# Mask additions laid out as one a chunk, equal score pieces side by side, and centring one batch later in a fused attention and gated FFN kernel

## The chip, the cores and the metric

The kernel runs on one core of a Trainium2 chip. A core has five engines that run their own instruction streams and wait for each other through semaphores: TensorE (PE, matmul, with its weight loads shown apart as PEld), VectorE (DVE), ScalarE (ACT), GpSimd (POOL) and SyncE (SP, which here issues DMA transfers). The metric is the device time of the whole program in microseconds (us).

## The reference

The input is x, 2048 tokens of 512 values. With xn = layernorm(x), the output is x + A(xn) * silu(B(xn)); A is sliding-window attention, B a gated feed-forward network. All weights are multiplied by 8.

```python
def _A_ref(x, wqkv, wo):                 # x: 1 x 2048 x 512
    H = 32; Dh = D // H; W = 256         # 32 heads of 16
    qkv = (x @ wqkv).reshape(B, S, 3, H, Dh).transpose(2, 0, 3, 1, 4)
    q, k, v = qkv[0], qkv[1], qkv[2]
    scores = jnp.einsum("bhqd,bhkd->bhqk", q, k) * (Dh ** -0.5)
    mask = (idx[:, None] - idx[None, :] >= 0) & (idx[:, None] - idx[None, :] < W)
    p = softmax(jnp.where(mask[None, None], scores, -1e9))
    o = jnp.einsum("bhqk,bhkd->bhqd", p, v)
    return o.transpose(0, 2, 1, 3).reshape(B, S, D) @ wo

def _B_ref(x, w1, w3, w2):               # F = 1792
    return (silu(x @ w1) * (x @ w3)) @ w2

xn = layernorm(x)
return x + _A_ref(xn, wqkv, wo) * silu(_B_ref(xn, w1, w3, w2))
```

## The kernel before

**Tiles.** The tokens are cut into four tiles t of 512; the 32 heads into four groups g of eight, and each group into two halves p of four heads. One (t, g, p) is a *unit* of attention: 32 units, eight of them in tile 0. Float32 products with the weights are made as three float16 products of high and low parts, so tensors come in pairs (XH and XL, wvh and wvl).

**A unit.** A first pass (L661 on PE, L675 on DVE) finds the largest score of each row. A second pass computes scores with the keys held in the array and the queries moving (`scores`, L742), adds masks to them on DVE (L749), exponentiates them on ACT (L752), and multiplies by the values (`values`, L770, float32). A unit of tiles 1 to 3 has five *chunks*, each filling one pair of PSUM banks of 2 x 512 columns: chunk 0 for both heads a of a row group, then two A chunks and two B chunks, one for each a. The chunk table CHUNKS gives, for each half h of the partitions, pieces (m, k, n, o, flag): key block m of 64 keys is multiplied with n blocks of 64 queries from block m + k on, and the result starts at block o of the chunk. Tile 0 has a table of its own, FIRST, with four chunks. The last tuple of a chunk lists its masks: at which block, every how many blocks, how many, and which entry of the constant table MK is added. MK holds triangles of 0 and a large negative number.

A score matmul uses a quarter of the array (64 x 64: half h, row group r), a value matmul an eighth (64 rows x 32 columns), so that four, or eight, run side by side. `values` takes the first piece of each half, then the second, and so on.

**The order of work.** PE's order is the order in which the code is written. A plan of batches puts the attention units between dense pieces: projections (L593, L563), gate and up of the FFN (L1032, L1257), the folded down projection (L1175) and the sum (L1309). The other engines' orders come from a scheduler that follows priorities; `urgent()` raises the priority of what is issued inside it, and `issue_after` names an instruction to stay behind. Queues hold work that is issued some steps later (`later`) or beside a batch: `behind` gives one work item to each batch of scores.

**Token statistics.** `prepare(t)` loads the four 128-token blocks of a tile, takes mean and variance on DVE (`stats`), computes the reciprocal root of the variance (`rstd`: a first guess on DVE, L442 to L447, then Newton steps, for tile 0 on DVE at L450 to L458, for later tiles as ten operations on POOL, L463 to L472), centres and scales the block on DVE (`centre`, L475), and transposes it on PE (`turn_beside`, L513). `prepare_beside` makes a list of these as work items. Also on DVE stand `L614`, which makes the low part of a projected tile, and L1281, which applies a scale to FFN results; the matmuls of L1257 use a slot or PSUM bank that such work has to free.

**The head.** For tile 0 the weights' powers of two are found first: sums of squares on ACT (L249), cast on DVE (L261), summed over partitions on PE, and turned into scales on DVE (L291 to L304). keep_busy (L1533) issues matmuls whose results nobody reads. Projected q and k go to DRAM (dQ, dK: L617 to L621) and come back in another layout (KA, qa: L637). L394 loads the raw weights of one head group, q and k.

Of the kernel before, what the change touches and what calls it, by code (L numbers as in the profile page):

```python
# [21 lines left out]
P = 128  # L22
# [47 lines left out]
AB = ((0,), (1,))  # L70
CHUNKS = (((0, 1), ((4, 0, 4, 0, 1),), ((-1, 1, 4, 0, 1),), ((0, 3, 2, 2, 0),)),
          *((a, ((0, 0, 5, 0, 1), (-2, 2, 3, 5, 1)), ((1, 0, 5, 0, 1), (5, 0, 3, 5, 1)),
             ((0, 4, 2, 0, 0), (5, 2, 2, 1, 0))) for a in AB),
          *((a, ((2, 0, 5, 0, 1), (6, 0, 2, 5, 1), (-4, 4, 1, 7, 1)), ((3, 0, 5, 0, 1), (7, 0, 1, 5, 1), (-3, 3, 2, 6, 1)),
             ((0, 4, 2, 0, 0), (5, 2, 2, 0, 0))) for a in AB))

FIRST = (*((a, ((0, 0, 5, 0, 1), (6, 0, 2, 5, 1), (4, 3, 1, 7, 1)), ((1, 0, 5, 0, 1), (5, 0, 3, 5, 1)),
            ((0, 4, 2, 0, 0), (5, 1, 1, 0, 0))) for a in AB),
         *((a, ((2, 0, 5, 0, 1), (4, 0, 3, 5, 1)), ((3, 0, 5, 0, 1), (7, 0, 1, 5, 1), (3, 1, 2, 6, 0)),
            ((0, 4, 2, 0, 0), (5, 1, 1, 0, 0))) for a in AB))  # L80


@with_exitstack
def tile_block(ctx: ExitStack, tc: tile.TileContext, x, wqkv, wo, w1, w3, w2, out):
# [124 lines left out]

    MK = const.tile([P, 3, 2, 64], BF16, name="MK")  # L210
    nc.vector.memset(MK[0:64], 0.0)
    for i, k in ((0, 0), (0, 1), (1, 1), (2, 0)):
        m = MK[0:64, i, k, :]
        nc.gpsimd.affine_select(m, m, pattern=[[-1 if k else 1, 64]], base=0, channel_multiplier=1 if k else -1,
                                compare_op=ALU.is_gt if k else ALU.is_ge, fill=NEG)

# [208 lines left out]
    def prepare(t):  # L425
# [14 lines left out]
        def rstd(b0, b1):  # L440
# [21 lines left out]
            u = lnpool.tile([P, b1 - b0], F32, name="u")  # L462
            pool.tensor_mul(sq, r0, r0)  # L463
            pool.tensor_mul(sq, sq, ve)
            pool.tensor_scalar(u, sq, -10 / 3, None, op0=ALU.add)
            pool.tensor_mul(sq, sq, u)
            pool.tensor_scalar(sq, sq, 5.0, None, op0=ALU.add)
            pool.tensor_mul(r0, r0, sq)
            pool.tensor_mul(sq, r0, r0)
            pool.tensor_mul(sq, sq, ve)  # L470
            pool.tensor_scalar(sq, sq, -0.5 * (3 / 8)**3 * XS, 1.5 * (3 / 8) * XS, op0=ALU.mult, op1=ALU.add)
            pool.tensor_mul(rs[:, b0:b1], sq, r0)  # L472

# [247 lines left out]
    def pass2(t, g, p):  # L721
# [3 lines left out]
        chunks = CHUNKS if t else FIRST  # L725

        def pieces(c):

# [7 lines left out]
        def scores(c):  # L736
            qa, ka = QA[t, g], keys(t, g)
            s = scores_bank()
            for o, h, a, (m, k, n, _, _) in pieces(c):
                for r in range(2):  # L740
                    rows = slice(64 * r, 64 * r + KR + 2)
                    nc.tensor.matmul(s[64 * h:64 * h + 64, r, o:o + 64 * n], ka[rows, 2 * p + a, 64 * (m + 4):64 * (m + 5)],  # L742
                                     qa[rows, 2 * p + a, 64 * (m + k):64 * (m + k + n)], start=True, stop=True)
            which, *_, masks = chunks[c]
            sv = s.rearrange("p r (a k q) -> p (r a) k q", a=len(which), q=64)
            for first, by, n, kind, of in masks:
                v = sv[:, :, first:first + by * (n - 1) + 1:by, :]
                with urgent():
                    nc.vector.tensor_add(v, v, MK[:, kind, of:of + n, :].unsqueeze(1).to_broadcast([P, 2 * len(which), n, 64]))  # L749
            cell[c] = pt = ppool.tile([P, 2, 512], F32, name="pt")  # L750
# [5 lines left out]
        def values(*cs):  # L756
# [8 lines left out]
            for group in zip_longest(*(turns[k] for k in sorted(turns))):  # L765
                for c, o, h, a, (m, k, n, _, _) in filter(None, group):
                    for r in range(2):
# [905 lines left out]
```

## Time and profile before

| | us |
|---|---|
| median of 3 runs (lowest, highest) | 818.14 (816.59, 819.52) |
| the profiled execution | 817.82 |
| its span in the profile | 816.0 |
| PE busy | 795.2 |
| DVE busy | 633.9 |
| ACT busy | 392.4 |
| POOL busy | 364.0 |

A row of the timeline reads: start in us, length in us, engine, line of the kernel, operation, output<-input by the program's names, the size of the array tile used (PE), the shape, the number of instructions in the row; in brackets the idle time ahead of it on its engine, and what ended it. Neighbouring instructions of one line stand in one row under the shape of the first, and the ends of matmuls overlap the starts of the next, so that for PE differences of starts are used. A row of the groups has, after the count, busy time and mean ns of one, and then the idle time before the group with what ended it. The stretches give busy time by engine and the granted clock of PE as a share of full speed.

### The profile page before, as it was taken

Reading aid. Unit: us, or ns where it says so; the run is one execution under the profiler, and the core shown is the slowest. Engines: PE = TensorE matmul, PEld = TensorE weight load, DVE = VectorE, ACT = ScalarE, POOL = GpSimd, SP = SyncE. Lnnn points to the kernel's source line nnn. Section 1 sums busy time; section 2 is a strip of 40 time slices with the busy share of each in tenths; the row PEclk is TensorE's granted clock in tenths of the full one; section 3 lists DMA queues with packets and bytes.
Section 4 is the critical chain, followed back from the end, with each engine's and each line's share of the span. In section 5 each row is a group of like instructions: output and inputs, shape, how many; then the busy total and the mean of one; then the engine's idle time right before and its main releaser. Section 6 shows DMA issues by size and latency. Waiting matters only on the chain.

```text
span 816.0 us, 23868 instructions
## 1 busy us (share of the span) xinstructions
PE 795.2 (97%) x9176; PEld 404.2 (50%) x9176; DVE 633.9 (78%) x2037; ACT 392.4 (48%) x591; POOL 364.0 (45%) x648
## 2 busy tenths in 40 slices
PE   8999989998999999999999999999999999999998
PEld 4434444443444444444444544456544654466465
DVE  8788788885898777787988888786777887775437
ACT  6879586563527444444444344434444334344421
POOL 2234266232328636434445264630246377560670
PEclk9999999999999999999999999999999999999999
DMA  9967554735457384666755544646362545325321
GB/s 284 258 218 254 165 179 130 276 115 188 136 141 255 105 267 120 215 180 208 204 169 171 172 100 144 168 128 189 122 197 74 161 127 149 111 77 181 111 56 70
DMA packets 109794, 134.18 MB, mean 164 GB/s; under 512 B 18864, under 2 KB 64880, under 8 KB 109680
## 3 DMA queue, kind: packets, MB, share of 16 engines
q1 hardware_dynamic: 109392, 132.13, 53.9%
q8 instruction: 72, 1.18, 0.6%
q10 hardware_dynamic: 288, 0.52, 0.2%
q14 instruction: 42, 0.34, 0.1%
HBM read 91.23 MB, written 36.57 MB: 157 GB/s over the span
## 4 chain that ended last, share of the span: by engine, by line
PE 78%; DVE 10%; ACT 5%; DMA 3%; issue 3%; SPq 1%; POOL 1%; DVEq 0%; POOLq 0%; ACTq 0%
PE m L1032 29%; PE po L770 8%; PE m L1257 8%; PE m L1175 8%; PE m L593 7%; PE s L742 5%; PE m L1309 4%; PE m L563 4%; PE s L661 3%; DVE junk L675 2%; PE po L661 2%; DMA slot<-in_A_x_dram 1%; DMA dW<-slot 1%; DVE s L749 1%; ACT slot L342 1%
## 5 line engine op out<-in xcount | busy, mean ns | idle before, releaser
L1032 PE MATMUL m<-XH,slot 128*128 128x512 f16 x896 | 267.5, 380 | 1.8 <-DVE slot L614 1.2
L752 ACT ACTIVATE pt<-s,es 128x1024 f32<-128x1024 f32 x152 | 167.6, 1112 | 198.6 <-DVE s L749 183.1
L339 POOL TENSOR_TENSOR slot<-slot,slot 128x256 f16<-128x256 f32 (+1 forms) x170 | 112.9, 691 | 218.2 <-ACT slot L1065 79.2
L1032 PEld LDWEIGHTS <-slot 128*128 128x128 f16 x1344 | 124.8, 98 | 156.2 <-issue 12.7
L1032 PE MATMUL m<-XL,slot 128*128 128x512 f16 x448 | 169.9, 379 | 0.0
L749 DVE TENSOR_TENSOR s<-s,MK 128x256 f32<-128x256 f32 (+2 forms) x280 | 118.7, 434 | 52.7 <-PE s L742 48.5
L675 DVE CUSTOM_DVE_ANT_0 junk<-s,MW 128x320 bf16<-128x320 f32 x276 | 133.9, 485 | 18.0 <-PE s L661 10.3
L675 DVE CUSTOM_DVE_ANT_0 junk<-po,MW 128x320 bf16<-128x320 f32 x172 | 83.4, 485 | 4.3
L1257 PE MATMUL m<-slot,slot 128*128 128x512 f16 x336 | 80.0, 385 | 3.6 <-DVE slot L614 3.2
L770 PE MATMUL po<-pt,V 64*32 64x320 f32 (+4 forms) x2880 | 77.2, 342 | 0.8 <-DVE pp L304 0.8
L593 PE MATMUL m<-XH,slot 128*128 128x512 f16 x240 | 71.0, 380 | 1.5 <-DVE slot L1051 0.8
L1175 PE MATMUL m<-slot,slot 128*128 128x256 f16 x588 | 68.4, 273 | 0.0
L1090 POOL TENSOR_TENSOR slot<-slot,slot 128x256 f16<-128x256 f32 x98 | 64.6, 671 | 1.1
L1047 ACT ACTIVATE slot<-m,sgs 128x512 f32<-128x512 f32 x56 | 38.3, 683 | 54.4 <-PE m L1032 53.1
L770 PEld LDWEIGHTS po<-pt,V 64*32 64x32 f32 x2880 | 50.5, 106 | 22.9 <-PE s L513 0.9
L1175 PEld LDWEIGHTS <-slot 128*128 128x128 f16 x588 | 56.1, 98 | 11.5 <-issue 2.8
L1051 DVE SCALAR_TENSOR_TENSOR slot<-slot,m 128x512 f32<-128x512 f32 x56 | 38.4, 685 | 27.9 <-ACT slot L1047 27.8
L742 PE MATMUL s<-qa,KA 50*64 50x320 f16 (+3 forms) x1472 | 58.6, 260 | 0.3 <-DVE M L675 0.2
L593 PEld LDWEIGHTS <-slot 128*128 128x128 f16 x384 | 35.6, 98 | 44.7 <-issue 3.3
L742 PEld LDWEIGHTS <-KA 50*64 50x64 f16 x1472 | 30.3, 106 | 52.5 <-issue 31.1
L1257 PEld LDWEIGHTS <-slot 128*128 128x128 f16 x336 | 30.9, 98 | 42.7 <-issue 8.9
L661 PE MATMUL s<-KA,qa 48*64 48x320 f16 (+3 forms) x824 | 45.1, 295 | 3.7 <-ACT pt L752 2.9
(188 smaller groups left out, 1095.3 us busy)
## 6 DMA issues: line engine op xcount, KB each, us to landing
slot<-dW SPq DMA_DIRECT2D x98, 256.0 KB
slot<-in_B_w_dram SPq DMA_DIRECT2D x56, 256.0 KB
slot<-dFold SPq DMA_DIRECT2D x48, 256.0 KB
dW<-slot SPq DMA_DIRECT2D x42, 256.0 KB
slot<-in_A_x_dram SPq DMA_DIRECT2D x30, 256.0 KB
KA<-dK SPq DMA_DIRECT2D x24, 288.0 KB
qa<-dQ SPq DMA_DIRECT2D x32, 192.0 KB
slot<-dWQ SPq DMA_DIRECT2D x24, 256.0 KB
```

The costliest lines, as they stand in the source:

```text
L339: op(out[:, c], a[:, c], b[:, c])
L593: nc.tensor.matmul(cell["pp"], w[:, (a * NC + c) * P:(a * NC + c + 1) * P], b[:, c, :], start=(c, i) == parts[0][0], stop=(c, i) == parts[ ...
L661: nc.tensor.matmul(s[c:c + w, r, :n], qa[rows, 2 * p + a, ii * P + c:ii * P + c + w], ka[rows, 2 * p + a, e - n:e], start=True, stop=True)
L675: lasts["maximum"] = nc.vector.tensor_tensor_reduce(out=junk[:, :n], in0=s[:, r, :n], in1=mask, scale=1.0, scalar=NEG, op0=ALU.add, op1=AL ...
L742: nc.tensor.matmul(s[64 * h:64 * h + 64, r, o:o + 64 * n], ka[rows, 2 * p + a, 64 * (m + 4):64 * (m + 5)], qa[rows, 2 * p + a, 64 * (m + k ...
L749: nc.vector.tensor_add(v, v, MK[:, kind, of:of + n, :].unsqueeze(1).to_broadcast([P, 2 * len(which), n, 64]))
L752: lasts["exp"] = nc.scalar.activation(pt, s, AF.Exp, scale=es)
L770: nc.tensor.matmul(cell["po"][32 * i:32 * i + 32, h, 64 * (m + k):64 * (m + k + n)], V[64 * h:64 * h + 64, (4 * t + m // 2) % VB, hd * VW: ...
L1032: nc.tensor.matmul(cell[k], w[:, (a * NC + c) * P:(a * NC + c + 1) * P], b[:, c, :], start=c == 0 and i == 0, stop=c == NC - 1 and i == 2)
L1090: nc.gpsimd.tensor_sub(lo, view, hi)
L1175: nc.tensor.matmul(cell["ps"][:, c], made[:, f:f + P], wj[:, g:g + 256], start=j == j0 and c == 0 and n == 0, stop=j == j1 - 1 and n == 2, ...
L1257: nc.tensor.matmul(ps, hh[:, a * TW + b * P:a * TW + (b + 1) * P], w[:, c * D:(c + 1) * D], start=f == f0 and i == 0, stop=f == f1 - 1 and ...
```

## The change

**Masks.** The mask table MK becomes eight entries of 64 columns, and each chunk's masks become one DVE addition: two places of n blocks each, against two runs of neighbouring entries of MK (chunk 0: one place). For that the blocks that need a mask have to lie next to each other, so some pieces are computed with their 64-query blocks in reverse order: a flag of -1 makes `turned_about` read the moving operand's blocks from last to first, in `scores` and again in `values`; outputs are written straight. In each unit of tiles 1 to 3 these are both heads' pieces of 256 columns of chunk 0 (half 1), a 192-column piece of each A chunk (half 0) and a 128-column piece of each B chunk (half 1). Tile 0's masks keep their shapes. The upper half of the table is built in MB on partitions 0 to 63 and copied by one DMA instead of three; POOL makes nine selections instead of four.

**B chunks.** The pieces of the B chunks stand in another order, so that in both halves they are 64, 320 and 128 columns wide.

**Statistics.** The ten POOL operations of `rstd` are issued as urgent, and for tiles 2 and 3 an empty work item stands between `rstd` and the first `centre`.

```diff
-CHUNKS = (((0, 1), ((4, 0, 4, 0, 1),), ((-1, 1, 4, 0, 1),), ((0, 3, 2, 2, 0),)),
-          *((a, ((0, 0, 5, 0, 1), (-2, 2, 3, 5, 1)), ((1, 0, 5, 0, 1), (5, 0, 3, 5, 1)),
-             ((0, 4, 2, 0, 0), (5, 2, 2, 1, 0))) for a in AB),
-          *((a, ((2, 0, 5, 0, 1), (6, 0, 2, 5, 1), (-4, 4, 1, 7, 1)), ((3, 0, 5, 0, 1), (7, 0, 1, 5, 1), (-3, 3, 2, 6, 1)),
-             ((0, 4, 2, 0, 0), (5, 2, 2, 0, 0))) for a in AB))
+CHUNKS = (((0, 1), ((4, 0, 4, 0, 1),), ((-1, 1, 4, 0, -1),), ((0, 1, 1, 7),)),
+          *((a, ((0, 0, 5, 0, 1), (-2, 2, 3, 5, -1)), ((1, 0, 5, 0, 1), (5, 0, 3, 5, 1)),
+             ((0, 4, 2, 0),)) for a in AB),
+          *((a, ((-4, 4, 1, 0, 1), (2, 0, 5, 1, 1), (6, 0, 2, 6, 1)), ((7, 0, 1, 0, 1), (3, 0, 5, 1, 1), (-3, 3, 2, 6, -1)),
+             ((0, 5, 2, 4),)) for a in AB))
...
+MASKS = ((1, 1), (0, 0), (2, 2), (2, 1), (2, 1), (1, 1), (2, 2), (1, 2))
...
+    MK = const.tile([P, len(MASKS), 64], BF16, name="MK")
+    MB = const.tile([64, len(MASKS), 64], BF16, name="MB")
+    for h, made in enumerate((MK[0:64], MB)):
+        nc.vector.memset(made, 0.0)
...
             pool = nc.gpsimd
             u = lnpool.tile([P, b1 - b0], F32, name="u")
-            pool.tensor_mul(sq, r0, r0)
...
+            with urgent():
+                pool.tensor_mul(sq, r0, r0)
...
         work.append(lambda: rstd(0, 4))
+        if t > 1:
+            work.append(lambda: None)
         work += [lambda bs=bs: [centre(b) for b in bs] for bs in pairs]
...
+        def turned_about(a, way):
+
+            return a.rearrange("p (n q) -> p n q", q=64)[:, ::-1, :] if way < 0 else a
...
                     nc.tensor.matmul(s[64 * h:64 * h + 64, r, o:o + 64 * n], ka[rows, 2 * p + a, 64 * (m + 4):64 * (m + 5)],
-                                     qa[rows, 2 * p + a, 64 * (m + k):64 * (m + k + n)], start=True, stop=True)
+                                     turned_about(qa[rows, 2 * p + a, 64 * (m + k):64 * (m + k + n)], way), start=True, stop=True)
...
-            sv = s.rearrange("p r (a k q) -> p (r a) k q", a=len(which), q=64)
-            for first, by, n, kind, of in masks:
-                v = sv[:, :, first:first + by * (n - 1) + 1:by, :]
+            sv = s.rearrange("p r (a w) -> p (r a) w", a=len(which))
+            for first, by, n, kind in masks:
+                places = 2 if by > 1 else 1
+                v = sv[:, :, 64 * first:64 * (first + n)]
+                if places == 2:
+                    v = type(v)(v.tensor, v.offset, [v.ap[0], v.ap[1], [64 * by, places], *v.ap[2:]])
+                    mk = MK[:, kind:kind + 2 * n, :].rearrange("p (i n) q -> p i (n q)", i=2)
+                else:
+                    mk = MK[:, kind:kind + n, :].rearrange("p n q -> p (n q)")
                 with urgent():
-                    nc.vector.tensor_add(v, v, MK[:, kind, of:of + n, :].unsqueeze(1).to_broadcast([P, 2 * len(which), n, 64]))
+                    nc.vector.tensor_add(v, v, mk.unsqueeze(1).to_broadcast([P, 2 * len(which), *mk.shape[1:]]))
...
-                                         cell[c][64 * h:64 * h + 64, r, o:o + 64 * n],
+                                         turned_about(cell[c][64 * h:64 * h + 64, r, o:o + 64 * n], way),
...
-    for i, k in enumerate((0, 2, 1)):
-        nc.sync.dma_start(MK[64:P, i], MK[0:64, k])
+    nc.sync.dma_start(MK[64:P], MB)
```

The lines of the changed kernel are up to 21 higher than those of the kernel before: `centre` is L484 there, `rstd` on POOL L472 to L481, the low part L625, the mask addition L770 and the value matmul L791. In the rows below an x and a count stand for so many such instructions in a row.

PE, the value matmuls of one unit of the later tiles, without their weight loads (po is the output, pt the exponentials, V the values). Before:

```order
L770 MATMUL po<-pt,V 32x256 x8
L770 MATMUL po<-pt,V 32x320 x8
L770 MATMUL po<-pt,V 32x192 x8
L770 MATMUL po<-pt,V 32x320 x8
L770 MATMUL po<-pt,V 32x128 x4
L770 MATMUL po<-pt,V 32x64 x8
L770 MATMUL po<-pt,V 32x128 x4
```

After:

```order
L791 MATMUL po<-pt,V 32x256 x8
L791 MATMUL po<-pt,V 32x320 x8
L791 MATMUL po<-pt,V 32x192 x8
L791 MATMUL po<-pt,V 32x64 x8
L791 MATMUL po<-pt,V 32x320 x8
L791 MATMUL po<-pt,V 32x128 x8
```

The pieces of 64 and 128 columns of the two halves no longer mix; the rest of PE's order stays, but for the score matmuls of the B chunks.

DVE, tile 2, around the first centring of its statistics (mv and rs are mean and reciprocal root). Before:

```order
L675 ISA junk,M<-po,M_106 128x256
L675 ISA M 128x1
L475 TENSOR_SCALAR slot_2653<-slot_2653,mv,rs 128x512
L614 SCALAR_TENSOR_TENSOR slot_3243<-m_3188,slot_3243 128x512
L1281 SCALAR_TENSOR_TENSOR slot_1458<-m_3248,dsc,slot_1458 128x512
L749 TENSOR_TENSOR s<-s,MK 128x4x64
```

After, at the same place:

```order
L686 ISA junk,M<-po,M_106 128x256
L686 ISA M 128x1
L625 SCALAR_TENSOR_TENSOR slot_3257<-m_3203,slot_3257 128x512
L1302 SCALAR_TENSOR_TENSOR slot_1473<-m_3262,dsc,slot_1473 128x512
L770 TENSOR_TENSOR s<-s,MK 128x4x64
```

The centring has left this place and stands behind a maximum of the next batch; the low part (L614, now L625) follows the maximum directly.

POOL, the second half of the ten operations for tile 2. Before:

```order
L467 TENSOR_SCALAR sq<-sq 128x4
L841 CAST slot_3259<-on 128x256
L468 TENSOR_TENSOR r_3152<-r_3152,sq 128x4
L841 CAST slot_3259<-on 128x256
L469 TENSOR_TENSOR sq<-r_3152 128x4
L339 TENSOR_TENSOR slot_3259<-on,slot_3259 128x256
L470 TENSOR_TENSOR sq<-sq,ve 128x4
L339 TENSOR_TENSOR slot_3259<-on,slot_3259 128x256
L471 TENSOR_SCALAR sq<-sq 128x4
L472 TENSOR_TENSOR rs<-sq,r_3152 128x4
```

After:

```order
L477 TENSOR_TENSOR r_3167<-r_3167,sq 128x4
L862 CAST slot_3273<-on 128x256
L478 TENSOR_TENSOR sq<-r_3167 128x4
L862 CAST slot_3273<-on 128x256
L479 TENSOR_TENSOR sq<-sq,ve 128x4
L347 TENSOR_TENSOR slot_3273<-on,slot_3273 128x256
L480 TENSOR_SCALAR sq<-sq 128x4
L347 TENSOR_TENSOR slot_3273<-on,slot_3273 128x256
L481 TENSOR_TENSOR rs<-sq,r_3167 128x4
```

The ten operations stand a place further ahead among the others; the last one still follows the two casts and the two L339 (now L347) operations.

DVE, the head, around the cast of the weights' sums (L261, now L269). Before:

```order
L447 TENSOR_SCALAR r_292<-r_292 128x4
L450 TENSOR_TENSOR sq<-r_292 128x4
L451 TENSOR_TENSOR sq<-sq,ve 128x4
L453 SCALAR_TENSOR_TENSOR sq<-sq 128x4
L454 SCALAR_TENSOR_TENSOR r_292<-sq,r_292 128x4
L261 CAST sb<-ssq 128x2
L456 TENSOR_TENSOR sq<-r_292 128x4
```

After:

```order
L269 CAST sb<-ssq 128x2
L458 TENSOR_TENSOR sq<-r_307 128x4
L459 TENSOR_TENSOR sq<-sq,ve 128x4
L299 TENSOR_SCALAR al<-s 128x1
L461 SCALAR_TENSOR_TENSOR sq<-sq 128x4
L306 TENSOR_SCALAR al<-al 128x1
L462 SCALAR_TENSOR_TENSOR r_307<-sq,r_307 128x4
```

The cast has moved ahead of the four Newton steps, and operations on the scale (al) stand between them.

SP, the head, around the first stores of dK and dQ. Before:

```order
L864 DMA slot_214<-in_B_w_dram 128x4x128
L621 DMA dK_147<-slot_408 128x512
L617 DMA dQ_143<-slot_417 128x2x512
L620 DMA dK_147<-slot_408 128x2x512
L618 DMA dQ_143<-slot_417 128x512
L394 DMA slot_551<-in_A_wqkv_dram 128x4x128
L621 DMA dK_148<-slot_462 128x512
```

After:

```order
L885 DMA slot_229<-in_B_w_dram 128x4x128
L402 DMA slot_566<-in_A_wqkv_dram 128x4x128
L402 DMA slot_567<-in_A_wqkv_dram 128x4x128
L632 DMA dK_164<-slot_423 128x512
L628 DMA dQ_160<-slot_432 128x2x512
L631 DMA dK_164<-slot_423 128x2x512
L629 DMA dQ_160<-slot_432 128x512
```

Two loads of weights now precede the stores; one of them stood right behind the four stores before, the other further on.

More of the change, by code (lines that the diff above doesn't have):

```diff
@@ L207, in tile_block @@
                             compare_op=ALU.is_ge, fill=NEG)
[L210 to L215, printed above, removed]
+    MK = const.tile([P, len(MASKS), 64], BF16, name="MK")
+    MB = const.tile([64, len(MASKS), 64], BF16, name="MB")
+    for h, made in enumerate((MK[0:64], MB)):
+        nc.vector.memset(made, 0.0)
+        kinds = [k[h] for k in MASKS]
+        for i, k in enumerate(kinds):
+            if k and (i == 0 or kinds[i - 1] != k):
+                n = next((j for j in range(i, len(kinds)) if kinds[j] != k), len(kinds)) - i
+                m = made[:, i:i + n, :]
+                nc.gpsimd.affine_select(m, m, pattern=[[0, n], [-1 if k == 2 else 1, 64]], base=0,
+                                        channel_multiplier=1 if k == 2 else -1,
+                                        compare_op=ALU.is_gt if k == 2 else ALU.is_ge, fill=NEG)
     NM = [const.tile([P, 64], F16, name=f"NM{i}") for i in range(3)]
@@ L738, in scores @@
             s = scores_bank()
-            for o, h, a, (m, k, n, _, _) in pieces(c):
+            for o, h, a, (m, k, n, _, way) in pieces(c):
                 for r in range(2):
@@ L765, in values @@
             for group in zip_longest(*(turns[k] for k in sorted(turns))):
-                for c, o, h, a, (m, k, n, _, _) in filter(None, group):
+                for c, o, h, a, (m, k, n, _, way) in filter(None, group):
                     for r in range(2):
```

22 lines of the change are left out of this document (11 added, 11 removed).

## The prediction, made before the changed kernel ran

> **What bounds the kernel now.** I read the page's busy line and chain first, then the stretches by stage, then single waits on the timeline.
>
> ```profile
> span 816.0 us, 23868 instructions
> PE 795.2 (97%) x9176; PEld 404.2 (50%) x9176; DVE 633.9 (78%) x2037; ACT 392.4 (48%) x591; POOL 364.0 (45%) x648
> PE 78%; DVE 10%; ACT 5%; DMA 3%; issue 3%; SPq 1%; POOL 1%; DVEq 0%; POOLq 0%; ACTq 0%
> ...
> 0.00:40.00 40.00, 36.16 (x201) 16.76 (x202) 31.74 (x112) 30.09 (x59) 11.29 (x41) 1.00 0.98 269
> 165.00:245.00 80.00, 75.38 (x831) 35.48 (x830) 65.16 (x232) 33.87 (x48) 22.80 (x44) 0.98 0.50 147
> 245.00:520.00 275.00, 274.78 (x3420) 131.16 (x3418) 223.92 (x699) 125.54 (x167) 141.64 (x246) 1.00 0.57 174
> 520.00:750.00 230.00, 229.81 (x2902) 128.98 (x2891) 173.43 (x536) 93.90 (x121) 103.40 (x174) 1.00 0.48 141
> ```
>
> The stretches list, after their length, the busy time of PE, its weight loads, DVE, ACT and POOL, then granted clock, DMA share and GB/s. From 245 to 750 us PE is busy 274.78 + 229.81 = 504.59 of 505.00 us. There only fewer or shorter PE instructions gain; a lighter DVE gains nothing. Before 245 PE has gaps, 4.62 us of them in the stretch from 165, and there order and waits count. So each part of the change is asked: does it shorten PE's own work, or close a gap before 245?
>
> **Part 1: the token statistics of tile 2.** The gap of the second stretch:
>
> ```profile
> 186.52 2.10 PE L1257 MATMUL m<-slot,slot 128*128 128x512 f16 x9
> 191.83 2.72 PE L1257 MATMUL m<-slot,slot 128*128 128x512 f16 x6 [3.20 <-DVE slot L614]
> ...
> 190.63 0.55 DVE L475 TENSOR_SCALAR slot<-slot,mv,rs 128x512 f32<-128x512 f32 x1 [3.40 <-POOL rs L472]
> 191.09 0.68 DVE L614 SCALAR_TENSOR_TENSOR slot<-m,slot 128x512 f16<-128x512 f32 x1
> ...
> 187.09 0.59 ACT L610 ACTIVATE slot<-m 128x512 f16<-128x512 f32 x1
> ...
> 190.40 0.20 POOL L472 TENSOR_TENSOR rs<-sq,r 128x4 f32<-128x4 f32 x1
> ...
> 191.80:194.60 2.80, 2.77 (x10) 0.84 (x13) 0.63 (x1) 0.00 (x0) 0.00 (x0) 0.50 0.70 233
> 133.96 1.40 PE m L1257 x6
> ```
>
> The DVE's first centring (L475) waits 3.40 us for the reciprocal root that POOL finishes at 190.60. Behind it in DVE's order stands L614, whose input ACT had ready at 187.09 + 0.59 = 187.68; PE waits for L614 and idles 3.20. Then the granted clock is 0.50, and six matmuls take 2.72 us; the same six took 1.40 in the chain's row at 133.96. So the wait costs 3.20 + 1.32 = 4.52 us.
>
> By the Trainium skill (TensorE: Matmul & The Clock Gate, Part 1: The HAM clock gate), the clock halves after an idle window of about 3.4 us and comes back after about as much busy time. The 0.50 of the row above agrees; nothing in the sum rests on this.
>
> The change puts the centring one work item, that is one batch of scores, later. The three batches between the first centring (190.63) and the fourth, which starts at 204.7, make 14.1 us, so one batch is about 4.7. The centring then comes at about 190.6 - 3.4 + 4.7 = 192 or later, after 190.60, and L614 can start at 187.7, before PE runs dry at 191.83 - 3.20 = 188.63: 187.7 + 0.68 = 188.4. What is late next is the transposes of tile 2, which start at 216.2: the fourth centring moves from 204.7 to about 209 and still precedes them. The urgent mark on POOL's ten operations leaves the last one behind the same four long operations, so I count nothing for it; if POOL still ended at 190.60, the batch of delay covers it alone. I take -4.5 (from -3.2, if the slow clock comes anyway, to -4.8).
>
> **Part 2: mask additions.** By shape, the groups of L749:
>
> ```profile
> L749 DVE TENSOR_TENSOR s<-s,MK 128x256 f32<-128x256 f32 x224 | 92.8, 427 | 52.5 <-PE s L742 48.5 <-issue 1.1 <-PE s L694 1.0
> L749 DVE TENSOR_TENSOR s<-s,MK 128x512 f32<-128x512 f32 x24 | 16.6, 691 | 0.0
> ```
>
> A unit of tiles 1 to 3 has eight additions of 427 ns and one of 691, 4.11 us; after, four of 691 and one of 427, 3.19 us. That is 0.92 x 24 = 22 us of DVE, and nothing on the path: PE is busy throughout 245 to 750, and DVE works 223.92 of 275.00 there. Tile 0 keeps its shapes. I take 0.
>
> **Part 3: values with equal pieces side by side (the B chunks).** One unit's value matmuls, row by row, and a change from 64-row tiles to the full array without it:
>
> ```profile
> 649.91 0.45 PE L770 MATMUL po<-pt,V 64*32 64x320 f32 x8
> 650.44 0.51 PE L770 MATMUL po<-pt,V 64*32 64x192 f32 x16
> 650.77 0.45 PE L770 MATMUL po<-pt,V 64*32 64x320 f32 x8
> 651.31 0.40 PE L770 MATMUL po<-pt,V 64*32 64x128 f32 x16
> 651.93 0.28 PE L1175 MATMUL m<-slot,slot 128*128 128x256 f16 x1
> ...
> 640.47 0.31 PE L661 MATMUL s<-KA,qa 48*64 48x320 f16 x4
> 640.62 0.30 PE L661 MATMUL po<-KA,qa 48*64 48x320 f16 x4
> 640.85 0.39 PE L1175 MATMUL m<-slot,slot 128*128 128x256 f16 x2
> ```
>
> Starts to starts: 320 columns 0.53, 192 equal columns 650.77 - 650.44 = 0.33, and the mixed last group (128 beside 64, then 64 beside 128; also 192 columns a half) 651.93 - 651.31 = 0.62. The last step holds the change to the full array: L661 alone takes 0.15 (640.47 to 640.62), followed by L1175 0.23 (to 640.85), so 0.08, at most 0.10. With equal pieces the group should take 0.33 + 0.10 = 0.43: -0.19 a unit, x 24 units = -4.6 us, all in stretches where PE is the bound. The least I allow is 0.12 (the small pieces keep a cost of their own), the most 0.24 (the 64-wide pieces hide in the long ones): -2.9 to -5.8.
>
> The Trainium skill (TensorE: Matmul & The Clock Gate, Part 3: Packing small matmuls) says that matmuls start and end strictly in program order. By it alone the mixed group would pay for 128 + 128 instead of 128 + 64 columns, 0.107 us at the 192-column row's rate, and the saving would be 2.6. The row's 0.62, against 0.43, says that more is lost, so I stay with 4.6.
>
> **Part 4: scores of the B chunks.** Two chunks' 24 score matmuls:
>
> ```profile
> 644.23 0.64 PE L742 MATMUL s<-qa,KA 50*64 50x320 f16 x24
> 644.76 0.33 PE L661 MATMUL po<-KA,qa 48*64 48x320 f16 x4
> ```
>
> They take 0.53; 1024 columns at the rate of the 512-column rows below (0.215) are 0.43. So at most 0.10 is to be had a unit (-2.4), and a narrow first piece could cost something: L661's 320 columns took 0.15 where 320 at that rate are 0.13, and that 0.02 to 0.03 a unit makes +0.7. I take 0, nearest the row: the work is the same.
>
> **Part 5: operands read back to front.** Chunk 0, A and B of every unit now read some moving operands in blocks of 64 columns from last to first. No row shows a reversed operand. The nearest is a matmul whose moving operand jumps back after every 128 columns (L1533 reads the same 128 columns four times), beside one that reads straight on:
>
> ```profile
> 12.79 1.02 PE L1533 MATMUL m<-onesb 128*128 128x512 bf16 x4 [0.58 <-DVE XL L499]
> 13.65 1.03 PE L593 MATMUL s<-XH,slot 128*128 128x512 f16 x4
> ```
>
> Four take 13.65 - 12.79 = 0.86, 0.215 each. L593's next group starts 0.86 later as well. Jumps cost nothing there; I take 0. The dear end is a rival below.
>
> **Part 6: the head.** DVE's order in the head changes, one cast (L261) standing ahead of the Newton steps:
>
> ```profile
> 8.25 0.19 ACT L249 ACTIVATION_READ_ACCUMULATOR sqa<-slot 128x1 f32 x1
> ...
> 7.95 0.16 DVE L450 TENSOR_TENSOR sq<-r 128x4 f32<-128x4 f32 x1
> 8.14 0.16 DVE L451 TENSOR_TENSOR sq<-sq,ve 128x4 f32<-128x4 f32 x1
> 8.62 0.16 DVE L261 CAST sb<-ssq 128x2 bf16<-128x2 f32 x1
> 9.57 1.91 DVE L475 TENSOR_SCALAR slot<-slot,mv,rs 128x512 f32<-128x512 f32 x4
> ```
>
> The cast needs ACT's sum, 8.25 + 0.19 = 8.44. Ahead of L450 it holds that back from 7.95 to about 8.5, and the rest of the chain goes 0.19 a step (7.95 to 8.14) as before; some of the scale operations between also move up. So centring starts 0.5 later, on the way to PE's first projection: +0.5.
>
> SP: three mask transfers become one, and two 256 KB weight loads (L394) that stood behind the first stores of dK and dQ now stand ahead of them.
>
> ```profile
> 21.41 1.34 SPq L394 DMA_DIRECT2D slot<-in_A_wqkv_dram  x1
> 24.62 0.82 SPq L637 DMA_DIRECT2D KA<-dK  x2
> 30.32 0.30 PE L661 MATMUL s<-KA,qa 48*64 48x128 f16 x7 [0.59 <-DMA qa<-dQ]
> 17.00:22.40 5.40, 5.40 (x30) 2.48 (x29) 5.40 (x18) 3.01 (x5) 0.00 (x0) 1.00 1.15 313
> 37.41 0.69 DVE L261 CAST sb<-ssq 128x2 bf16<-128x2 f32 x1 [0.96 <-ACT sqa L249]
> 39.78 1.33 ACT L333 ACTIVATE slot<-slot,sw 128x512 f16<-128x512 f32 x2 [1.82 <-DVE sw L302]
> ```
>
> 512 KB at 269 to 313 GB/s are 1.7 to 1.9 us. If the stores and the fetch of KA behind them land that much later, the first scores' wait of 0.59 grows by up to 1.9; the waits of 0.96 and 1.82 downstream can swallow it again. Between 0 and +1.9 I take +0.5, as the later waits are about as long. Mask building itself (nine selections on POOL for four, one more memset on DVE) is covered by POOL's 11.29 busy of 40 us. Sum of the head: +1.0, from 0 to +2.5.
>
> **Sum.** -4.5 - 4.6 + 0 + 0 + 1.0 = -8.1. The profiled execution took 817.82 us (span 816.0), so 817.82 - 8.1 = 809.7; its time is 0.3 under the median of the runs, 818.14, which I leave out as noise.
>
> **Rivals.**
> *Reversed operands stream slowly (slower).* At half rate a unit pays again for its reversed columns. Values take both chunks of a kind at once: 256 + 192 + 128 = 576 column times of 0.53 / 320 = 1.66 ns, 0.96 us. Scores go a head at a time, 2 x 576 = 1152 columns of 0.42 ns (0.215 / 512), 0.48. Together 1.44 x 24 = 35 us, and 809.7 + 35 = 845. It decides the sign from a quarter of that, 8.1 of 35. Against it are the two rows at 12.79 and 13.65. A page of the Trainium skill (Advanced Engine Details and Errata, Memory Cachelines) warns that non-contiguous access slows matmuls where PSUM is read, and asks for repeated hits on 16-byte lines in SBUF; runs of 64 elements in SBUF keep those hits, and no run here shows a reversed one.
> *The stall moves.* DVE's wait goes, but another operand (the centring now beside the next batch) stops PE there: -4.6 + 1.0 = -3.6, 814.2.
> *Small pieces cost the same anywhere.* The 0.19 is the price of 64-column groups, whose weight loads don't hide, not of the mixture: -4.5 + 1.0 = -3.5, 814.3.
> *Both, so that nothing is left:* +1.0, 818.8.
>
> **How the numbers follow.** Forecast 0.64; the stall moves 0.09; small pieces 0.10; both 0.05; slow reversal 0.12. The forecast's own bounds: -4.8 - 5.8 - 2.4 + 0 = -13.0 (804.8) and -3.2 - 2.9 + 0.7 + 2.5 = -2.9 (814.9). The range 805.0 to 815.0 holds these and the next two rivals, about 0.82. A measurement tells about 0.3% (2.5 us) from no change: faster is the forecast and most of the two rivals at 814 (0.80), the same "both" and the rest of them (0.07), slower the reversal and a dear head (0.13).
>
> **What the profile after would show.** Right: no wait of L475 on POOL near 190 and no 0.50 clock behind it; the value groups at 0.11, 0.53 and 0.21 + 0.1 instead of 0.53 and 0.62; L749's 128x512 group x96 at about 691 ns; PE's busy time from 245 to 750 lower by 3 to 5 us for the same work. Wrong: score or value matmuls of the reversed pieces with longer steps (rival one); a new PE gap at 188 to 200, or the first KA fetch several us later than 24.62, which would make the head dearer than all I gave it.

## The result and the profile after

The changed kernel takes 814.92 us (median of 7 runs, 814.23 to 815.96) against 818.14 (816.59 to 819.52): a ratio of 0.9962, 95% interval 0.9952 to 0.9972, or 3.2 us less. The forecast was 8.1 us less. Its profiled execution took 815.93 us.

The page of the changed kernel, and the stretches that the prediction used:

```profile
span 813.8 us, 23773 instructions
PE 794.9 (98%) x9176; PEld 409.6 (50%) x9176; DVE 624.1 (77%) x1942; ACT 392.9 (48%) x591; POOL 365.4 (45%) x653
...
165.00:245.00 80.00, 78.58 (x871) 37.35 (x869) 68.66 (x250) 38.31 (x54) 24.10 (x47) 1.00 0.54 163
245.00:520.00 275.00, 273.56 (x3415) 133.21 (x3413) 219.30 (x640) 123.87 (x165) 140.74 (x245) 1.00 0.56 171
520.00:750.00 230.00, 229.83 (x2899) 132.09 (x2897) 167.38 (x490) 94.67 (x122) 103.58 (x174) 1.00 0.49 141
```

The stretch from 165 has filled up: PE 78.58 of 80 us, formerly 75.38, and the granted clock is 1.00. The stretch from 245 has lost 1.2 us of PE's busy time, which is a new gap, not less work. DVE is 10 us lighter.

The place of the old wait, PE, DVE and POOL in the changed kernel:

```profile
188.39 3.40 PE L1278 MATMUL m<-slot,slot 128*128 128x512 f16 x15
...
189.58 0.69 DVE L625 SCALAR_TENSOR_TENSOR slot<-m,slot 128x512 f16<-128x512 f32 x1 [0.49 <-ACT slot L621]
195.02 0.54 DVE L484 TENSOR_SCALAR slot<-slot,mv,rs 128x512 f32<-128x512 f32 x1
...
192.25 0.20 POOL L481 TENSOR_TENSOR rs<-sq,r 128x4 f32<-128x4 f32 x1
```

L1278 (L1257 before) now runs 15 matmuls without a gap where it ran 9, waited 3.20 us and ran 6 at half the clock. L625 waits only for ACT; POOL ends at 192.25 + 0.20 = 192.45, and the centring comes at 195.02, when its input has long been there.

The values of one unit. The rows give the start of a group: 256 columns, the 192-column group of the A chunks, the 64-column group, and the dense matmul behind the unit (17 matmuls under way, 16 of them of 64 columns and the first of 320):

```profile
647.49 0.62 PE L791 MATMUL po<-pt,V 64*32 64x256 f32 x16
648.46 0.51 PE L791 MATMUL po<-pt,V 64*32 64x192 f32 x16
648.79 0.54 PE L791 MATMUL po<-pt,V 64*32 64x64 f32 x17
649.95 0.28 PE L1196 MATMUL m<-slot,slot 128*128 128x256 f16 x1
```

The 192-column group, half of it read in reverse, takes 648.79 - 648.46 = 0.33, as before. The B chunks take 649.95 - 648.79 = 1.16. Before, they took 651.93 - 650.77 = 1.16 as well: nothing was gained. The forecast for the three groups was 0.11, 0.53 and 0.31; by their first starts in the trace (648.787, 648.899, 649.437, and 649.954 for the dense matmul) they take 0.11, 0.54 and 0.52.

The mask additions have the count and length that were worked out, 96 at 694 ns. Added up, the lengths of all mask additions fall from 121.6 to 99.9 us. DVE's busy time falls by 9.8 only, for the records of neighbouring instructions overlap (all of DVE's add up to 749.8 us before, where 633.9 are busy):

```profile
L770 DVE TENSOR_TENSOR s<-s,MK 128x512 f32<-128x512 f32 x96 | 64.8, 694 | 50.6 <-PE s L757 50.5
L770 DVE TENSOR_TENSOR s<-s,MK 128x256 f32<-128x256 f32 x56 | 23.8, 424 | 4.4 <-PE s L757 3.4 <-PE s L705 1.0
```

And two waits of PE are new or longer, one in the head and one near 331 us:

```profile
26.69 0.33 SPq L648 DMA_DIRECT2D KA<-dK  x1
31.89 0.24 PE L672 MATMUL s<-KA,qa 48*64 48x128 f16 x1 [1.88 <-DMA qa<-dQ]
...
329.11 0.69 DVE L1325 SCALAR_TENSOR_TENSOR slot<-slot,slot 128x512 f32<-128x512 f32 x1 [0.17 <-ACT slot L1324]
329.72 0.48 DVE L686 CUSTOM_DVE_ANT_0 junk<-po,MW 128x320 bf16<-128x320 f32 x1
330.13 0.75 DVE L1334 SCALAR_TENSOR_TENSOR slot<-m,us,slot 128x512 f32<-128x512 f32 x1
330.80 0.48 DVE L686 CUSTOM_DVE_ANT_0 junk<-po,MW 128x320 bf16<-128x320 f32 x1
331.34 0.33 PE L672 MATMUL po<-KA,qa 48*64 48x320 f16 x4 [1.14 <-DVE M L686]
```

Because PE's instructions stand in nearly the same order in both kernels, the start of each can be set against its start before. This table is worked out from the two traces, in us, plus meaning later:

```
PE at (time before)   after minus before   what happened
10.3                  +0.5                 centring 0.5 later (9.57, now 10.06)
29.5                  +2.4                 first fetch of KA 26.69 instead of 24.62
32.2                  +3.7                 half clock behind that wait
55.6                  +2.0                 before waits 1.03 here, after does not
194.8                 -2.9                 the wait of tile 2 is gone: -4.8 from 187 to 197
318                   -3.0                 value groups shift inside a unit, nothing stays
333                   -1.9                 the new wait of 1.14
end of PE's work      -2.4
```

From 55.6 us on these are steps of -0.2 up to 187 us, -4.8 at tile 2, +1.1 near 331, and small ones both ways behind it that add up to -0.5.

### The profile page after: what moved, and what is told of

Read it like the earlier page. It is cut to its first block, busy times and chain, and to the rows that moved or that the text cites. A ratio compares the mean times of both kernels' runs of the same rounds, so it can differ in the third digit from the quotient of the medians.

```text
span 813.8 us, 23773 instructions
## 1 busy us (share of the span) xinstructions
PE 794.9 (98%) x9176; PEld 409.6 (50%) x9176; DVE 624.1 (77%) x1942; ACT 392.9 (48%) x591; POOL 365.4 (45%) x653
## 4 chain that ended last, share of the span: by engine, by line
PE 79%; DVE 9%; DMA 5%; ACT 4%; issue 2%; SPq 1%; POOL 0%; DVEq 0%; ACTq 0%; POOLq 0%
PE m L1053 30%; PE po L791 8%; PE m L1278 8%; PE m L1196 8%; PE m L604 7%; PE s L757 5%; PE m L574 4%; PE m L1330 4%; PE s L672 3%; DVE junk L686 2%; PE po L672 2%; DMA slot<-in_A_wqkv_dram 1%; DMA slot<-in_A_x_dram 1%; DVE s L770 1%; ACT pt L773 1%
## 5 line engine op out<-in xcount | busy, mean ns | idle before, releaser
L347 POOL TENSOR_TENSOR slot<-slot,slot 128x256 f16<-128x256 f32 (+1 forms) x170 | 113.0, 692 | 219.9 <-ACT slot L1086 86.0
L770 DVE TENSOR_TENSOR s<-s,MK 128x512 f32<-128x512 f32 (+2 forms) x184 | 97.9, 543 | 55.2 <-PE s L757 53.9
L1278 PE MATMUL m<-slot,slot 128*128 128x512 f16 x336 | 78.7, 380 | 0.6 <-DVE slot L1072 0.4
L791 PE MATMUL po<-pt,V 64*32 64x320 f32 (+4 forms) x2880 | 77.2, 342 | 0.8 <-DVE pp L312 0.8
L791 PEld LDWEIGHTS po<-pt,V 64*32 64x32 f32 x2880 | 57.0, 106 | 16.4 <-PE s L522 0.9
L757 PE MATMUL s<-qa,KA 50*64 50x320 f16 (+2 forms) x1472 | 58.2, 259 | 0.3 <-DVE M L686 0.2
L757 PEld LDWEIGHTS <-KA 50*64 50x64 f16 x1472 | 27.8, 106 | 51.7 <-issue 35.0
L1077 DVE SCALAR_TENSOR_TENSOR slot<-m,slot 128x512 f32<-128x512 f32 x56 | 38.5, 687 | 15.8 <-PE m L1053 15.6
L1278 PEld LDWEIGHTS <-slot 128*128 128x128 f16 x336 | 30.7, 98 | 39.0 <-issue 4.7
```

The lines of the kernel that those rows point to most:

```text
L347: op(out[:, c], a[:, c], b[:, c])
L770: nc.vector.tensor_add(v, v, mk.unsqueeze(1).to_broadcast([P, 2 * len(which), *mk.shape[1:]]))
L791: nc.tensor.matmul(cell["po"][32 * i:32 * i + 32, h, 64 * (m + k):64 * (m + k + n)], V[64 * h:64 * h + 64, (4 * t + m // 2) % VB, hd * VW: ...
L1278: nc.tensor.matmul(ps, hh[:, a * TW + b * P:a * TW + (b + 1) * P], w[:, c * D:(c + 1) * D], start=f == f0 and i == 0, stop=f == f1 - 1 and ...
```

## The experiments

All compare with the kernel before on the same chip. Theory M is the prediction's (unequal pieces side by side cost time); theory W was formed from the trace after (a short group costs time because the weight loads of the group behind it don't fit into it).

**The delay alone.** The kernel before, with the empty work item and nothing else:

```diff
         work.append(lambda: rstd(0, 4))
+        if t > 1:
+            work.append(lambda: None)
```

> The kernel before, with one part of the change alone: an empty work item between the statistics and the first centring of tiles 2 and 3. Nothing else differs but the place of the centrings in DVE's order. Theory A (the wait for POOL's reciprocal root costs 3.2 us of PE and 1.3 to 1.4 us of halved clock, and one batch of delay removes all of it): 4.5 to 5 us less than before, about 813.4; L1257 at about 187 without idle time, granted clock 1.00 after it. Rival B (the wait only moves to the next batch): within 1 us of before. If A holds, the delay alone gains more than the whole change did (3.2 us).

Measured: 813.02 us, ratio 0.9945 (0.9933 to 0.9957), 5.0 less than before. PE at the old wait, L1257 being L1259 here:

```profile
186.51 3.40 PE L1259 MATMUL m<-slot,slot 128*128 128x512 f16 x15
...
190.39 0.20 POOL L472 TENSOR_TENSOR rs<-sq,r 128x4 f32<-128x4 f32 x1
```

POOL is as late as before (190.39 + 0.20 = 190.59, then 190.60), and nobody waits for it. Theory A holds. This one edit gains more than the whole change: by difference, the rest of the change costs 1.8 us.

**Equal pieces alone.** The kernel before, with the pieces of the B chunks reordered:

```diff
-... ((2, 0, 5, 0, 1), (6, 0, 2, 5, 1), (-4, 4, 1, 7, 1)), ((3, 0, 5, 0, 1), (7, 0, 1, 5, 1), (-3, 3, 2, 6, 1))
+... ((-4, 4, 1, 7, 1), (2, 0, 5, 0, 1), (6, 0, 2, 5, 1)), ((7, 0, 1, 5, 1), (3, 0, 5, 0, 1), (-3, 3, 2, 6, 1))
```

> The kernel before, with the pieces of the B chunks alone in the changed kernel's order, 64, 320, 128 columns in both halves; masks, their additions and all places in PSUM as before, no reversed operand. Theory M, the prediction's (unequal pieces side by side cost 0.19 us a unit): 4.6 us less than before, the B chunks' value matmuls 0.97 us instead of 1.16. Theory W (the cost is that of the weight loads behind a short group: 8 loads about 17 ns apart, 0.14 us, against 64 or 128 columns, 0.05 or 0.11 us a pass; where the short group stands in the middle, the next group starts late): no gain, within 0.5 us of before, 1.16 us as before, and the 320-column matmuls behind the 64-column ones start about 17 ns apart over 0.18 us.

Measured: 817.91 us, ratio 0.9997 (0.9986 to 1.0008). The B chunks' values, from the first 64-column matmul to the dense one behind:

```profile
649.32 0.54 PE L770 MATMUL po<-pt,V 64*32 64x64 f32 x17
650.48 0.28 PE L1175 MATMUL m<-slot,slot 128*128 128x256 f16 x1
```

1.16 us again, and the 320-column matmuls behind the 64-column ones start over 0.183 us (649.427 to 649.610), as theory W said. Theory M falls.

The trace of this run shows one thing more. The wait of tile 2 is in it, for nothing was done about it, but the granted clock behind it is 1.00, and the six matmuls take 1.46 us where the kernel before had 2.72:

```profile
191.83 1.46 PE L1257 MATMUL m<-slot,slot 128*128 128x512 f16 x6 [3.20 <-DVE slot L614]
```

So the wait of 3.20 is there every time it was looked at, and the half clock behind it only in some executions. The 5.0 of the delay alone is a difference of medians and holds both.

**The small group last.** The kernel before with a single exchange, the second and third piece of half 1, which makes the order 320, 128, 64 in both halves:

```diff
-... ((3, 0, 5, 0, 1), (7, 0, 1, 5, 1), (-3, 3, 2, 6, 1))
+... ((3, 0, 5, 0, 1), (-3, 3, 2, 6, 1), (7, 0, 1, 5, 1))
```

> As the last one, but with the order 320, 128, 64 in both halves: equal pieces again, the shortest group last, so that no group of eight tiles has to load its weights behind it. Theory M: the same as the order 64, 320, 128, for the pieces are equal in both. Theory W: faster than that order by 0.05 to 0.15 us a unit, 1 to 4 us in 24 units, as only the 128-column group is too short for the loads behind it; the value matmuls of the B chunks take 1.02 to 1.11 us.

Measured: 815.45 us, ratio 0.9971 (0.9962 to 0.9981), 2.6 less than before.

```profile
648.81 0.72 PE L770 MATMUL po<-pt,V 64*32 64x320 f32 x16
649.35 0.48 PE L770 MATMUL po<-pt,V 64*32 64x128 f32 x21
649.87 0.28 PE L1175 MATMUL m<-slot,slot 128*128 128x256 f16 x1
```

649.87 - 648.81 = 1.06 instead of 1.16. In all 24 units the traces agree to 3 ns: 1.059 to 1.060 us here, 1.165 to 1.168 in the kernel before. 0.107 us a unit makes 2.6 us, the whole gain. How the eight tiles of a 320-column group start, as the traces have it (us; a float32 matmul leaves two records, called passes here, and this is the first):

```
changed kernel, behind 64 columns:   648.899  648.982  648.999  649.015  649.032  649.049  649.065  649.082
  the weight loads of the last seven:         648.978  648.994  649.011  649.028  649.044  649.061  649.078
this kernel, behind 192 columns:     648.806  648.810  648.812  648.815  648.820  648.823  648.825  648.829
```

Behind the 192-column group the eight start within 0.023 us. Behind the 64-column group seven of them come late and 17 ns apart, the last 0.183 us behind the first, and each starts 4 to 5 ns after its own weight load. Eight loads at 17 ns are 0.14 us, an estimate; a pass of 64 columns lasts 0.056 us (648.787 to 648.843), one of 192 columns 0.16 (648.462 to 648.624). The lateness is carried to the end of the unit: the last group's first passes, behind it, also start over 0.206 us (649.437 to 649.643).

**The small group in the middle.** 320, 64, 128 in both halves:

> The kernel before, B chunks alone in the order 320, 64, 128 in both halves: equal pieces, the long group first as in the faster order, the 64-column group in the middle. Theory W: the 128-column group behind it starts late, so nothing is gained, within 0.7 us of before. Rival (the long group first is what gains): 2 us or more less than before, about 815.5.

Measured: 817.98 us, ratio 0.9998 (0.9986 to 1.0009).

```profile
652.61 0.72 PE L770 MATMUL po<-pt,V 64*32 64x320 f32 x16
653.77 0.28 PE L1175 MATMUL m<-slot,slot 128*128 128x256 f16 x1
```

1.16 us. The rival falls: the long group first is not what gains. The three orders in which the 64-column matmuls have another group of eight behind them cost the same, whether mixed with 128 columns or not (1.165 to 1.168 us in every unit of these traces); only those that put them last are shorter. What the runs show is the effect of the place; that it is the loads that hold the next group back is read from the records, where each late matmul follows its load.

**The changed kernel with the small group last:**

> The changed kernel with the pieces of the B chunks in the order 320, 128, 64 instead of 64, 320, 128, and nothing else. Theory W: 2.0 to 2.7 us less than the changed kernel, 812.2 to 812.9, the value matmuls of the B chunks about 0.11 us shorter a unit. Theory M: no different from the changed kernel, 814.9.

Measured: 812.8 us, ratio 0.9931 (0.9917 to 0.9944), 2.1 less than the changed kernel. The B chunks take 1.06 here too:

```profile
645.39 0.72 PE L791 MATMUL po<-pt,V 64*32 64x320 f32 x16
646.45 0.28 PE L1196 MATMUL m<-slot,slot 128*128 128x256 f16 x1
```

**The head.** The changed kernel with the copy of the masks in three transfers, which puts SP's order back:

```diff
-    nc.sync.dma_start(MK[64:P], MB)
+    for i, j in ((0, 3), (3, 6), (6, 8)):
+        nc.sync.dma_start(MK[64:P, i:j], MB[:, i:j])
```

> The changed kernel, with the copy of the upper masks split into three transfers again. The two loads of raw weights go back behind the first store of dK and behind the stores of the first group, as in the kernel before; DVE's head, with the cast ahead of the Newton steps, stays as changed. Theory S (the stores of dK and dQ were held back by the two loads: PE waits 1.88 + 0.46 us instead of 0.59 for the first scores, then loses about 1.3 us to a halved clock): 1.5 to 3 us less than the changed kernel, about 812.5; the first fetch of KA near 25.1 instead of 26.69 us. Rival (the order of the head is made up for later, as 1.7 us of it were between 51 and 56 us): within 0.8 us of the changed kernel.

Measured: 815.51 us, ratio 0.9973 (0.9963 to 0.9983), no less than the changed kernel. In its trace KA is fetched at 26.18, and PE is 2.5 us ahead of the changed kernel at 36 us, then 0.2 ahead at 57: it waits there for DVE (0.76 us for L625). The 2.5 holds a half clock on either side, near 11 to 15 us in this execution and near 33 to 36 in the changed kernel's. Theory S is right that the long wait for the first scores goes, and wrong about the total.

**The head, all of it.** As the last, and MB set to zero on POOL; DVE, ACT and SP then keep the old order in the first 60 us:

```diff
-        nc.vector.memset(made, 0.0)
+        (nc.gpsimd if h else nc.vector).memset(made, 0.0)
```

> The changed kernel with the three transfers of the last experiment, and with MB set to zero on POOL rather than on DVE. With these, SP, DVE and ACT go through the first 60 us in the order of the kernel before (the cast behind the four Newton steps, the three sums of squares near 41 to 56 us where they were). The three transfers alone took 2.5 us off by 36 us and had given them back by 57, where PE waits for DVE. Theory H (the head's 2.0 us at 57 us come from the changed order on DVE and ACT): about 2 us less than the changed kernel, 813, and PE at the L1053 that stands at 57.69 us in the changed kernel near 55.7. Rival (the halved clock near 12 us or the transfers decide, whatever the order of the engines): 814.5 to 815.5, no different from the changed kernel.

> The changed kernel with the head's order as before, once more, for a second profiled execution. If the halved clock near 10.4 to 13.3 us belongs to this order, it is there again and PE stands 1.0 us behind the kernel before at 57 us; if not, PE keeps step with the kernel before up to 180 us.

Measured: 814.76 and 814.57 us in two series, ratios 0.9967 (0.9954 to 0.9979) and 0.9959 (0.9946 to 0.9972). That is 0.2 to 0.35 less than the changed kernel, not 2. The two profiled executions of this one kernel differ, 10 to 14 us of the first and then of the second:

```profile
10.00:14.00 4.00, 3.61 (x18) 3.27 (x19) 3.47 (x7) 2.53 (x5) 0.00 (x0) 0.60 1.14 308
...
10.00:14.00 4.00, 3.03 (x21) 2.26 (x22) 3.72 (x8) 3.43 (x7) 0.00 (x0) 1.00 1.12 305
```

With the clock at 0.60 the execution took 815.42 us, without 814.56; in the second one PE keeps step with the kernel before to within 0.2 us up to 180 us. So the halved clock there does not belong to the order, and it is worth about 1 us.

The head is not all that differs between this kernel and the changed one. From 60 us to the end PE gains 4.4 us on the kernel before in the changed kernel's profiled execution, and 3.8 in both executions here: in the second of them the wait near 331 us is 1.28 instead of 1.14, and another of 0.33 for a row maximum stands at 508. So the 0.2 to 0.35 is not the price of the head alone.

**The changed kernel again**, for a second profiled execution:

> The changed kernel once more, for a second profiled execution. If the halved clock near 31 to 36 us follows from the longer wait for the first scores, it is there again; if it is a matter of where the wait falls in a given execution, it may be missing, and the execution is then about 1.3 us nearer to the kernel before at 36 us.

Measured: 814.92 us, ratio 0.9963 (0.995 to 0.9976); the profiled execution took 815.70. The half clock near 32 to 36 us is there again, and PE is 1.9 us behind at 55.6. But both profiled executions are among the slowest of their series (815.93 of 814.23 to 815.96, 815.70 of 814.22 to 815.70). In this series two executions have a mean granted clock of 1.00 and take 814.22 and 814.36 us, the two others 0.998 and 815.48 and 815.70. So the half clock, which costs about 1.3 us, is not in every execution, and the 2.0 us of the table need not be there in the median. What the head costs in the median stays open.

**Two additions a chunk.** The changed kernel with each two-place mask of tiles 1 to 3 split:

```diff
-                with urgent():
-                    nc.vector.tensor_add(v, v, ...)
+                apart = places == 2 and t > 0
+                for i in range(2 if apart else 1):
+                    vi, mi = (v[:, :, i], mk[:, i]) if apart else (v, mk)
+                    with urgent():
+                        nc.vector.tensor_add(vi, vi, ...)
```

> The changed kernel with each two-place mask of tiles 1 to 3 put on by two additions of 128x256 instead of one of 128x512, at the same places. DVE gets back 96 additions, 96 x (2 x 0.427 - 0.694) = 15 us. Theory D (the lighter DVE gains nothing, but its order changed: near 330 us two FFN operations of 0.69 and 0.75 us stand ahead of a row maximum, for which PE waits 1.14): about 1.1 us less than the changed kernel, 813.8, and no wait of L672 near 331 us. Rival (fewer additions do save time somewhere): slower than the changed kernel, 815.5 or more.

Measured: 814.06 us, ratio 0.9954 (0.9941 to 0.9966), 0.9 less than the changed kernel, though DVE's additions are 15 us longer in sum (its busy time is 629.2 us, 5.1 more). PE at the place of the new wait, and at another place:

```profile
328.92 0.64 PE L757 MATMUL s<-qa,KA 50*64 50x64 f16 x24
329.62 0.33 PE L672 MATMUL po<-KA,qa 48*64 48x320 f16 x4
...
532.37 2.75 PE L1333 MATMUL m<-slot,slot 128*128 128x512 f16 x12 [0.48 <-DVE slot L1075]
```

The wait of 1.14 is gone, and the two maxima stand ahead of the two FFN operations again: theory D is right about this place. Its size is not shown. A wait of 0.48 us that the changed kernel does not have stands at 532, and from 60 us to the end PE gains 4.6 us on the kernel before, against 4.4 in the changed kernel. The rest of the difference between the two profiled executions lies in the head, where this edit changes nothing: PE waits 1.21 us for the first scores instead of 1.88. The intervals of the medians overlap as well.

**What is worth keeping.** The kernel before with the delay and the small group last, and a variant with 128 ahead of 320:

> The kernel before with the empty work item and, in the B chunks, the second and third piece of half 1 exchanged (320, 128, 64 in both halves); everything else as before. If the two gains lie in different stretches and add up: 818.0 - 5.0 - 2.6 = 810.4. If one takes from the other: 811.5 to 813.

> The same with the order 128, 320, 64 in both halves. Theory W in its plain form (a group costs what the loads of the next exceed its last pass): 192 columns before the 128, 0.16 us, still cover the loads; 128 before the 320 is short by as much as 128 before the 64 in the other order. So within 0.7 us of the order 320, 128, 64. If the loads of the last group before the dense matmuls count too, it is the same in both.

Measured: 810.59 us, ratio 0.9912 (0.9897 to 0.9927), and 811.23, ratio 0.992 (0.9906 to 0.9934). The two gains add up to the forecast of 810.4. The second order costs the same in the values, 1.06 us a unit in both traces. Its 0.64 us more are within what was allowed; in its trace stands a wait that the other does not have:

```profile
530.24 2.75 PE L1311 MATMUL m<-slot,slot 128*128 128x512 f16 x12 [0.62 <-DVE slot L1053]
```

The faster of the two beats both kernels, without the mask table, the reversed operands or the new head:

```profile
span 808.9 us, 23868 instructions
PE 792.2 (98%) x9176; PEld 404.5 (50%) x9176; DVE 633.0 (78%) x2037; ACT 392.3 (49%) x591; POOL 364.0 (45%) x648
```

## Why the prediction was right or wrong

The sign was right and the size was not: 3.2 us instead of 8.1. The step that failed is **part 3**, the -4.6 for equal value pieces.

- *Part 1* (-4.5): right in mechanism. Alone it measured -5.0. The wait of 3.20 is the sure part of it; the half clock behind it, 1.3 us of the sum, comes in some executions and not in others (0.50 in the kernel before, 1.00 behind the same wait in the run with equal pieces). The low end of -3.2 covers that in size. The idle window of about 3.4 us of the Trainium skill (TensorE: Matmul & The Clock Gate, Part 1: The HAM clock gate), with which the prediction took its row to agree, does not fit the runs as it stands: besides that 1.00, the changed kernel's clock halves near 33 us behind waits of 1.88 and 0.46 with matmuls between them. The urgent mark was not needed: without it the wait is gone as well.
- *Part 2* (0): the additions were costed rightly, and a lighter DVE gained nothing that can be told from noise. What was left out is that fewer additions let the scheduler order the other DVE work differently: L1325 and L1334 slipped between two row maxima, and PE waits 1.14 us. With the additions split this wait goes and another comes elsewhere, so what part 2 costs in sum is not shown.
- *Part 3* (-4.6): measured 0 when made alone (817.91 us, and 1.16 us a unit as before). The row was read rightly, 0.62 where 0.43 would do, but the 0.19 was put down to 128 beside 64 columns. It belongs to the short groups wherever another group of eight stands behind them, because that group's weight loads don't fit into their pass. That is the rival "small pieces cost the same anywhere", which was given 0.10 and 814.3 us; only its "anywhere" is wrong, as the last place is cheaper. The trace of before held the answer: the starts of the last group, looked at one by one rather than as a total, are spaced out (its last four at 651.683, 651.700, 651.718 and 651.733), where the eight of the long group ahead start within 0.023 us (650.769 to 650.792). The rule of the Trainium skill that was weighed there (TensorE: Matmul & The Clock Gate, Part 3: Packing small matmuls) gave 2.6; that too counted on equal pieces and did not come. By chance 2.6 is what the order 320, 128, 64 gains, for another reason. Nor do the starts of the mixed group follow the order of the program, which has four of 128 columns and then four of 64: 128 and 64 start in turn (651.307, 651.311, 651.313, 651.316).
- *Part 4* (0): right. The two B chunks' scores take 0.468 us in most units before and 0.471 after. The 0.53 that the prediction read is of a unit that takes longer than most, so there was less to be had than its 0.10.
- *Part 5* (0): right. The reversed 192 columns take 0.33 us as the straight ones did, and the score matmuls of chunk 0 and of the A chunks 0.24 as before, so the 845 us rival is out.
- *Part 6* (+1.0): each wait came, the DVE step to 0.01 us (+0.49) and the fetch of KA a little above the upper bound of 1.9 (26.69 instead of 24.62, +2.07). What was left out is the half clock behind that wait, 1.7 us in the profiled execution (+2.3 to +3.9 between 30 and 37 us). There 2.0 us are left at 57 us; in executions without the half clock it should be about 0.7, an estimate from the 1.3 us between the two pairs of times above.

In the profiled executions the parts add up by the table: +2.0 in the head, -0.2, -4.8, 0 in the values, +1.1 near 331 and -0.5 behind it make -2.4 at the end of PE's work. (In time these two executions are 1.9 us apart, the medians 3.2; the changed kernel's profiled one is among the slowest of its series.) Against the forecast, part 3 is missing whole (4.6 us), the head costs 1.0 more and the new wait 1.1. Of the separate runs on the changed kernel only the small group last (-2.1) is clear of the noise. What the head and the additions cost in the median stays open.

## What to carry to other kernels

When small matmuls are packed into tiles of the array, cost a group by the weight loads of the group behind it as well as by its columns, and put the shortest group where no full set of loads follows; here that was worth 0.107 us a unit. When a stall is found, try the one edit that moves the waiting instruction before anything else: one line gained more here than the whole change. Taking work off an engine that isn't the bound changes the scheduler's order, and with it small waits of the bound engine come and go (here 1.14 us near 331, and with the additions split 0.48 at 532); compare the orders at the places where the bound engine is fed.

## What the runs showed of the hardware

Weight loads of eight 64 x 32 tiles behind a pass of 64 float32 columns were worked off 17 ns apart, and the matmuls started over 0.183 us; behind 192 columns they started within 0.023 us. Moving operands read in blocks of 64 from last to first took as long as straight ones (0.33 us for a group of 192 float32 columns, 0.24 us for a chunk's f16 scores). And the granted clock near 10 to 14 us was 0.60 in one execution and 1.00 in another of the same kernel, at 0.9 us of its time; behind the same wait of 3.20 us it was 0.50 in one kernel and 1.00 in another with the same order there. So a half clock in a single profiled execution can't be put down to a change.
